# A new order of all recorded steps in a fused attention and gated-MLP kernel

## The chip, the core and the metric

The kernel runs on one core of one Trainium2 chip. The metric is the device time of one execution in microseconds (us), taken on the chip. The core has five engines that work side by side, each through its own queue of instructions and in that queue's order: TensorE (PE in the profile; its weight loads are listed apart as PEld), VectorE (DVE), ScalarE (ACT), GpSimd (POOL) and SyncE (SP). Transfers are started by two queues here: SP starts "hardware" DMAs (q1 in the profile), POOL starts "software" DMAs (q0), and both are carried by the same 16 DMA engines of the core. POOL also computes; a POOL instruction that waits holds up every load that stands behind it.

## The reference

Four batches of 768 rows, 8 heads of 64, go through windowed attention with four sink columns; the result, with heads laid side by side (512 columns), goes through a gated MLP whose gate mixes rows.

```python
scores = q @ k.T / 8                      # per batch and head, 768 x 768
keep = (col < 4) | ((row - col >= 0) & (row - col < 128))
a = softmax(where(keep, scores, -1e9))
x = (a @ v) as [batch, 768, 512]
h = gelu_tanh(x @ w_in)                   # w_in 512 x 1024
u, v = h[..., :512], h[..., 512:]
v_n = (v - mean) / sqrt(var + 1e-6) * g_ln
v_s = w_sg @ v_n + b_sg                   # w_sg 768 x 768, mixes rows
out = x + (u * v_s) @ w_out               # w_out 512 x 512
```

Only tiles on the diagonal of the score matrix, the tiles next to it and the sink columns are computed.

## The kernel before, in words

The kernel is a list of short step names, the string `STEPS`. A loop at the end of the kernel goes through it and calls the function of each name; each function records a few instructions, and no scheduler reorders them. So the place of a step in the list fixes its place in the queue of every engine that it uses, and nothing but data dependencies, buffers coming free and these queues decides when it runs. A step's numbers are, as a rule, batch, then head pair or tile group; a last letter names the engine (A ScalarE, D VectorE, P GpSimd).

How one batch goes through:

- **Loads.** Batch 0's q and k come in four head pairs each, by SP, as plain float32 (`LPQ`, `LPK`, 384 KB each, line 245), and are cast to bfloat16 by a compute engine (`CPQ`, `CPK`, lines 199, 200 and 204). Batches 1 to 3 have q and k loaded and cast by POOL's DMAs, six tiles of 128 rows each (`LQ`, `LK`, line 225); every batch's v comes in two halves by POOL (`LVH`, line 271, 384 KB each, four heads a half). The weights are POOL's loads too: `LW.0` and `LW.1` are the two halves of w_in (line 277), `LWS` the halves of w_sg, `LB` the bias, `LWO` w_out. `LC` brings the sink rows of v by SP.
- **Turns.** q and k have to be transposed. `TQ` and `TK` do it on TensorE into PSUM (lines 376 and 382), and `EQ`, `EK` copy the result to SBUF. For batch 0 a turn is one head pair over all rows; for batches 1 and 2 it is two tiles of rows. Batch 3's six turns are DMA transposes on SP instead (`DQ`, `DK`, line 440).
- **Attention.** `QK` computes the scores of one head pair and one third of the rows (line 483; a biased one adds the mask with line 478), `EX` exponentiates (line 488), `MK` masks on VectorE (line 495) or GpSimd (lines 498 and 501), `KS`, `SK` and `SX` do the sink columns, `AV` multiplies with v (lines 524 to 531), `NR` divides by the row sums. `SK` reads the turned q of all four head pairs.
- **Between.** x is transposed for the MLP: `XT` with the copy `XE` for batch 0, DMA transposes `XD` on SP (line 557) for the others.
- **MLP.** `MV` and `MU` compute the two halves of h (lines 566 and 607), `GV` and `GU` are the gelu, `BN`, `RS`, `NM`, `Z` the normalisation, `SP` the row mixing (line 627), `GT` and `GM` the gate, `OU` or `OH` the output product (lines 644 and 657), `RA` or `RH` add x, `ST` and `SH` store by SP.
- **Fillers.** `HM.n` puts n matmuls on zeros ahead of the next PSUM tile; `TBL` touches ScalarE so that its function table is loaded at that place.

Rings of buffers bound how far an engine may run ahead: two for scores, four for other PSUM tiles, two each for q, k and v. Batch 2 takes the q, k and v buffers of batch 0. A DMA semaphore is used again by the eighth software DMA after it, which waits for the earlier one to land.

The start of the two queues that transfers hang on, and of TensorE's, before:

```
POOL  MASK VSK IDEN CPK.1.P LVH.0.0 LVH.0.1 CPK.3.P LQ.1.0 LQ.1.1 LW.0 LK.1.0 LW.1 MK.0.2.1.P ...
SP    LPQ.0 LPK.0 LPK.1 LPQ.1 LPQ.2 LG LPK.2 LPK.3 LPQ.3 LC ...
PE    TQ.0.0 TK.0.0 QK.0.0.0 QK.0.0.1.1 QK.0.0.2.1 TK.0.1 TQ.0.1 TQ.0.2 QK.0.1.0 QK.0.1.1.1 TK.0.2 TK.0.3 TQ.0.3 ...
```

Of the kernel before, what the change touches and what calls it, by code (L numbers as in the profile page):

```python
# [25 lines left out]
MK.0.1.0.D SX.0.1 SX.0.2 QK.0.3.1 MK.0.2.1.P GCP.D NR.0.0.0 EX.0.3.0 AV.0.0.1 AV.0.1.0 AV.0.1.1 NR.0.0.1 EX.0.3.1
QK.0.1.2 NR.0.1.0 AV.0.2.0 AV.0.3.0 EX.0.1.2 MK.0.3.1.P NR.0.1.1 QK.0.2.2 AV.0.2.1 NR.0.2.0 EX.0.2.2 TQ.1.0 NR.0.3.0
MK.0.1.2.P QK.0.3.2 AV.0.3.1 EQ.1.0.A NR.0.2.1 XT.0.0 NR.0.3.1 LWS.0 AV.0.0.2 EX.0.3.2 TBL.G AV.0.1.2 XE.0.0.D LK.1.1
XT.0.1 MK.0.2.2.D MV.0.0 XE.0.1.A LK.1.2 NR.0.0.2 MK.0.3.2.D LK.1.3 NR.0.1.2 AV.0.2.2 AV.0.3.2 LQ.1.2 NR.0.2.2 GV.0.0
MV.0.1 NR.0.3.2 LQ.1.3 BN.0.0 LWS.1 XT.0.2 GV.0.1 MU.0.1 XE.0.2.A BN.0.1 WT.0 GU.0.1 TK.1.0 MV.0.2 RS.0.1 EK.1.0.A  # L30
LK.1.4 NM.0.1 WE.0.A WT.1 GV.0.2 LK.1.5 TK.1.1 MU.0.2 LB.P EK.1.1.A BN.0.2 Z.0.0.A LK.2.0 WT.2 GU.0.2 MU.0.0 WE.1.D
RS.0.2 WE.2.D Z.0.1.A LQ.2.0 NM.0.2 Z.0.2.A Z.0.3.D Z.0.4.D WT.3 LQ.2.1 WT.4 GU.0.0 TBL.E WE.3.D WT.5 LQ.1.4 Z.0.5.D
TQ.1.1 QK.1.0.0 EQ.1.1.D QK.1.1.0 LQ.1.5 SP.0.0.0 WE.4.D LK.2.1 EX.1.0.0 VSM.1 SP.0.0.1 WE.5.D EX.1.1.0 LVH.1.0
GT.0.0.0 TK.1.2 KS.1 GT.0.0.1 QK.1.2.0 QK.1.3.0 EX.1.2.0 SP.0.0.2 LVH.1.1 GM.0.0.0.D EX.1.3.0 MK.1.2.0.D TQ.2.0
EK.1.2.A LQ.2.2 QK.1.0.1 EQ.2.0.D QK.1.1.1 TQ.1.2 EX.1.0.1 GT.0.0.2 LWO SP.0.0.3 EQ.1.2.D EX.1.1.1 LK.2.2 MK.1.0.1.D
TK.2.0 MK.1.0.0.D QK.1.2.1 LK.2.3 EK.2.0.A QK.1.3.1 MK.1.3.0.D SK.1.0 GM.0.0.1.D LQ.2.3 SP.0.1.0 EX.1.2.1 GT.0.0.3
MK.1.1.0.D LQ.2.4 EX.1.3.1 SP.0.1.1 MK.1.1.1.D LQ.2.5 MK.1.2.1.D SX.1.0 QK.1.0.2 QK.1.1.2 GT.0.1.0 EX.1.0.2 GM.0.0.2.P
SP.0.1.2 GT.0.1.1 EX.1.1.2 LK.2.4 GM.0.1.0.D AV.1.0.0 MK.1.3.1.D AV.1.1.0 LK.2.5 GM.0.0.3.D QK.1.2.2 GT.0.1.2 QK.1.3.2
EX.1.2.2 SP.0.1.3 NR.1.0.0 MK.1.1.2.P EX.1.3.2 NR.1.1.0 AV.1.2.0 AV.1.3.0 MK.1.0.2.P GT.0.1.3 QK.2.0.0 QK.2.1.0
NR.1.2.0 EX.2.0.0 OU.0.0 MK.1.2.2.P NR.1.3.0 TK.2.1 RA.0.0 AV.1.0.1 XD.1.0 EK.2.1.A MK.1.3.2.P AV.1.1.1 NR.1.0.1  # L40
AV.1.2.1 EX.2.1.0 GM.0.1.2.P NR.1.1.1 AV.1.3.1 NR.1.2.1 QK.2.2.0 LK.3.0 QK.2.3.0 EX.2.2.0 OU.0.1 NR.1.3.1 GM.0.1.3.P
EX.2.3.0 TBL.G OU.0.2 XD.1.1 RA.0.1 GM.0.1.1.P TK.2.2 MK.2.3.0.D TQ.2.1 LVH.2.0 TQ.2.2 EQ.2.1.D MV.1.0 EQ.2.2.D LQ.3.0
EK.2.2.D LQ.3.1 VSM.2 MU.1.0 GV.1.0 MK.2.1.0.D LVH.2.1 BN.1.0 MV.1.1 GU.1.0 LQ.3.2 RA.0.2 LQ.3.3 MK.2.0.0.D MV.1.2
GV.1.1 MK.2.2.0.D LK.3.1 KS.2 LK.3.2 BN.1.1 MU.1.1 GV.1.2 LK.3.3 BN.1.2 RS.1.1 MU.1.2 GU.1.1 LQ.3.4 NM.1.1 Z.1.0.A
RS.1.2 OU.0.3 GU.1.2 TBL.E LQ.3.5 NM.1.2 Z.1.1.D SK.2.0 Z.1.4.D QK.2.0.1 Z.1.2.D Z.1.3.A QK.2.1.1 Z.1.5.D OU.0.4
RA.0.3 DK.3.0 SP.1.0.0 RA.0.4 SX.2.0 EX.2.0.1 SP.1.0.1 GT.1.0.0 DQ.3.0 EX.2.1.1 GM.1.0.0.D SP.1.1.0 MK.2.0.1.P
GT.1.0.1 QK.2.2.1 ST.0.3 GT.1.1.0 QK.2.3.1 GM.1.0.1.P DQ.3.1 EX.2.2.1 AV.2.0.0 SP.1.1.1 MK.2.1.1.D EX.2.3.1 MK.2.2.1.P
NR.2.0.0 AV.2.1.0 QK.2.0.2 DQ.3.2 QK.2.1.2 KS.3 EX.2.0.2 MK.2.3.1.P NR.2.1.0 SP.1.1.2 GT.1.1.1 EX.2.1.2 OU.0.5
MK.2.0.2.P GT.1.1.2 ST.0.0 ST.0.4 QK.2.2.2 RA.0.5 QK.2.3.2 MK.2.1.2.P EX.2.2.2 AV.2.2.0 AV.2.3.0 NR.2.2.0 SP.1.1.3
EX.2.3.2 NR.2.3.0 QK.3.0.0 MK.2.3.2.P QK.3.1.0 GT.1.1.3 XD.2.0 EX.3.0.0 AV.2.0.1 MK.2.2.2.D AV.2.1.1 EX.3.1.0 NR.2.0.1  # L50
AV.2.2.1 GM.1.1.3.P ST.0.1 NR.2.1.1 AV.2.3.1 ST.0.2 ST.0.5 GM.1.1.0.P SK.3.0 NR.2.2.1 QK.3.2.0 QK.3.3.0 NR.2.3.1
EX.3.2.0 GM.1.1.2.P SP.1.0.2 EX.3.3.0 XD.2.1 SP.1.0.3 GT.1.0.2 SX.3.0 TBL.G MK.3.3.0.D MV.2.0 GM.1.0.2.P DK.3.1
GM.1.1.1.D LK.3.4 MK.3.0.0.D OU.1.3 LVH.3.0 GV.2.0 OU.1.4 RA.1.3 LVH.3.1 OU.1.5 ST.1.3 RA.1.4 GT.1.0.3 MV.2.1 ST.1.4
MK.3.1.0.D LK.3.5 BN.2.0 GM.1.0.3.P MV.2.2 GV.2.1 BN.2.1 MU.2.1 GV.2.2 BN.2.2 RS.2.1 MU.2.0 GU.2.1 NM.2.1 RA.1.5
RS.2.2 MU.2.2 GU.2.0 NM.2.2 Z.2.4.D Z.2.5.D Z.2.0.A Z.2.1.D OU.1.0 GU.2.2 TBL.E Z.2.2.D MK.3.2.0.D OU.1.1 RA.1.0
Z.2.3.D QK.3.0.1 QK.3.1.1 RA.1.1 SP.2.0.0 EX.3.0.1 DK.3.2 EX.3.1.1 OU.1.2 MK.3.0.1.P GT.2.0.0 ST.1.5 VSM.3 ST.1.0
QK.3.2.1 ST.1.1 QK.3.3.1 EX.3.2.1 SP.2.1.0 GM.2.0.0.D MK.3.1.1.P RA.1.2 EX.3.3.1 SP.2.0.1 ST.1.2 MK.3.3.1.P QK.3.0.2
GT.2.0.1 QK.3.1.2 EX.3.0.2 SP.2.1.1 GT.2.1.0 MK.3.2.1.P EX.3.1.2 GM.2.1.0.D SP.2.1.2 GT.2.1.1 GM.2.0.1.D AV.3.0.0
MK.3.1.2.P GT.2.1.2 AV.3.1.0 NR.3.0.0 AV.3.2.0 AV.3.3.0 MK.3.0.2.P NR.3.1.0 QK.3.2.2 QK.3.3.2 EX.3.2.2 SP.2.0.2
NR.3.2.0 NR.3.3.0 EX.3.3.2 TBL.G SP.2.0.3 MK.3.2.2.P GT.2.0.2 XD.3.0 AV.3.0.1 GT.2.0.3 MK.3.3.2.P AV.3.1.1 NR.3.0.1  # L60
AV.3.2.1 GM.2.0.3.P NR.3.1.1 AV.3.3.1 SP.2.1.3 GM.2.0.2.D GM.2.1.1.P NR.3.2.1 OU.2.0 NR.3.3.1 GT.2.1.3 XD.3.1 OU.2.1
RA.2.0 GM.2.1.3.P OU.2.2 GM.2.1.2.D SH.2.0.0 SH.2.0.1 RA.2.1 MV.3.0 RA.2.2 SH.2.1.0 SH.2.1.1 OU.2.3 GV.3.0 OU.2.4
BN.3.0 MV.3.1 RA.2.3 RA.2.4 MV.3.2 SH.2.3.0 SH.2.3.1 GV.3.1 SH.2.2.0 SH.2.2.1 SH.2.4.0 SH.2.4.1 BN.3.1 OU.2.5 GV.3.2
MU.3.2 BN.3.2 RS.3.1 MU.3.1 GU.3.2 NM.3.1 RS.3.2 NM.3.2 Z.3.0.D Z.3.1.A MU.3.0 Z.3.2.D Z.3.3.A Z.3.4.A Z.3.5.D RA.2.5
SH.2.5.0 SH.2.5.1 SP.3.1.0 GU.3.0 SP.3.1.1 GU.3.1 GT.3.1.0 SP.3.1.2 GM.3.1.0.D GT.3.1.1 SP.3.1.3 GM.3.1.1.D GT.3.1.2
# [650 lines left out]
```

## Time and profile before

The median of three runs is 155.65 us (155.44 to 155.72). The execution that was profiled took 155.89 us; its span from the first to the last instruction is 154.2 us, so 1.7 us lie around the span.

| stretch of the span, us | what runs there | TensorE busy | VectorE | ScalarE | GpSimd |
|---|---|---|---|---|---|
| 0 to 24 | attention of batch 0, first loads | 21.05 of 24 | 16.59 | 19.63 | 17.06 |
| 24 to 55 | MLP of 0, attention of 1 | 30.74 of 31 | 26.32 | 27.90 | 26.21 |
| 55 to 90 | MLP of 1, attention of 2 | 33.63 of 35 | 29.72 | 23.39 | 30.50 |
| 90 to 124 | MLP of 2, attention of 3 | 33.84 of 34 | 29.54 | 20.95 | 22.25 |
| 124 to 150 | MLP of 3 | 25.95 of 26 | 19.61 | 8.15 | 3.67 |

Busy times of an engine say whether it had an instruction in flight; for TensorE they also hold short fillings of the pipeline. The granted clock of TensorE is 1.00 in all stretches.

### The profile page before, as it was taken

To read this page: it belongs to the slowest core of one execution; us is meant where nothing else is said; L and a number is where in the kernel's file an instruction comes from. 1 tells how busy PE (TensorE), PEld (TensorE's weight loads), DVE (VectorE), ACT (ScalarE), POOL (GpSimd) and SP (SyncE) were. 2 spreads that over 40 slices of the span, in tenths; PEclk is the share of its full clock that TensorE was granted. 3 is DMA by queue.
4 is the path that set the end of the run, shared out by engine and by line. 5 is a ranking of instruction groups with operands and counts; after the bars stand their busy time and mean duration, and the time that the engine had idled before them with its cause. 6 is when DMAs were issued, how large, how long until landed. Compare 5 with 4: busy or idle time off the path is not lost.

```text
span 154.2 us, 3867 instructions
## 1 busy us (share of the span) xinstructions
PE 145.7 (95%) x1540; PEld 94.5 (61%) x1554; DVE 122.9 (80%) x296; ACT 100.0 (65%) x117; POOL 99.7 (65%) x127
## 2 busy tenths in 40 slices
PE   6899899999999988999899999999999999999990
...
DMA  4999999999999999999999399996510582410055
GB/s 158 305 351 157 154 195 204 166 189 211 148 141 154 185 155 140 147 150 156 156 223 250 81 276 177 185 190 81 211 72 1 105 221 73 150 54 20 0 203 206
DMA packets 87178, 24.67 MB, mean 160 GB/s; under 512 B 78772, under 2 KB 84920, under 8 KB 87160
## 3 DMA queue, kind: packets, MB, share of 16 engines
...
q14 instruction: 6, 0.05, 0.1%
...
## 4 chain that ended last, share of the span: by engine, by line
PE 54%; POOL 18%; DMA 15%; ACT 4%; DVE 4%; issue 2%; SPq 1%; DVEq 0%; ACTq 0%; POOLq 0%
PE mm L627 15%; DMA v_sb<-in_v_dram 11%; PE mm L644 10%; PE sc L566 9%; PE sc L607 8%; POOL q L225 5%; POOL k L225 4%; DMA uT<-in_k_dram 4%; PE sc L483 4%; PE mm L524 3%; POOL v_sb L271 3%; PE mm L528 2%; POOL wsg_gated L637 2%; POOL P L498 2%; POOL P L501 2%
## 5 line engine op out<-in xcount | busy, mean ns | idle before, releaser
L488 ACT ACTIVATE P<-sc 128x1024 bf16<-128x1024 f32 (+1 forms) x48 | 43.4, 952 | 10.3 <-PE sc L483 10.1
L627 PE MATMUL mm<-wsgT,z 128*128 128x384 bf16 x192 | 34.4, 327 | 0.3 <-ACT z L597 0.3
L627 PEld LDWEIGHTS <-z 128*128 128x128 bf16 x192 | 17.6, 98 | 12.5 <-issue 0.7
L570 ACT ACTIVATE vt<-sc 128x1024 f32<-128x1024 f32 x12 | 12.3, 1027 | 18.4 <-PE sc L566 18.4
L632 DVE SCALAR_TENSOR_TENSOR gtmp<-mm,g_sb,b_bc 128x384 bf16<-128x384 f32 x32 | 19.0, 610 | 4.2 <-PE mm L627 4.0
L637 POOL TENSOR_TENSOR wsg_gated<-gtmp,uT 128x384 bf16<-128x384 bf16 x15 | 14.9, 1006 | 11.3 <-DVE gtmp L632 11.2
L607 PE MATMUL sc<-xT,w_in_sb 128*128 128x256 bf16 x192 | 22.1, 273 | 0.0
L566 PE MATMUL sc<-w_in_sb,xT 128*128 128x512 bf16 x92 | 21.8, 379 | 0.2
L644 PE MATMUL mm<-w_out_sb,wsg_gated 128*128 128x512 bf16 x85 | 21.2, 379 | 0.5
L498 POOL TENSOR_SCALAR_AFFINE_SELECT P<-P 128x512 bf16<-128x512 bf16 x21 | 13.7, 653 | 11.4 <-ACT P L488 11.4
L607 PEld LDWEIGHTS <-w_in_sb 128*128 128x128 bf16 x192 | 18.7, 98 | 2.9
L579 DVE BATCH_NORM_STATS2 st<-vt 128x6 f32<-128x512 f32 x24 | 15.4, 685 | 6.1 <-ACT vt L570 6.0
L541 DVE TENSOR_TENSOR x_sb<-mm,rcp 128x384 bf16<-128x384 f32 (+1 forms) x36 | 18.5, 513 | 1.2
L588 POOL TENSOR_TENSOR rs<-rs,neg_half 128x4 f32<-128x4 f32 (+1 forms) x8 | 7.1, 882 | 15.8 <-DVE rs L583 14.4
L225 POOL DMA_DIRECT2D k<-in_k_dram x18 | 16.4, 924 | 1.3 <-DMA v_sb<-in_v_dram 1.3
L648 DVE TENSOR_TENSOR ot<-mm,x_sb 128x512 f32<-128x512 f32 x23 | 15.4, 683 | 2.2 <-PE mm L644 2.2
L225 POOL DMA_DIRECT2D q<-in_q_dram x18 | 16.8, 956 | 0.0
L524 PE MATMUL mm<-v_sb,P 128*128 128x65 bf16 x192 | 16.1, 194 | 0.6 <-DVE x_sb L541 0.4
L524 PEld LDWEIGHTS <-P 128*128 128x128 bf16 x192 | 14.5, 97 | 2.5 <-DMA v_sb<-in_v_dram 0.6
L528 PE MATMUL mm<-v_sb,P 128*128 128x65 bf16 x160 | 15.4, 193 | 0.4 <-POOL P L501 0.4
L612 ACT ACTIVATE uT<-sc 128x1024 bf16<-128x1024 f32 x12 | 12.2, 1024 | 5.1 <-PE sc L607 5.1
L566 PEld LDWEIGHTS <-xT 128*128 128x128 bf16 x96 | 9.2, 98 | 10.1
...
## 6 DMA issues: line engine op xcount, KB each, us to landing
...
```

Source lines behind the costliest of these rows:

```text
L225: return nc.gpsimd.dma_start(out=dst.rearrange("p (h d) -> p h d", h=H), in_=heads(src, b, i))
L488: nc.scalar.activation(out=P.new((b, p, g))[:, :, 0:w], in_=sc_ring[b, p, g][:, :, 0:w], func=AF.Exp, scale=scale)
L498: nc.gpsimd.affine_select(out=p4[:, :, :, 0:128], in_=p4[:, :, :, 0:128], compare_op=ALU.is_ge, fill=0.0, base=0, pattern=[[0, 2], [0, 2], ...
L524: nc.tensor.matmul(av[:, il, hl, :], pt[:, hl, c:c + 128], vb[:, h, i, :], start=first, stop=False)
L528: nc.tensor.matmul(av[:, il, hl, :], pt[:, hl, c:c + 128], vb[:, h, i - 1, :], start=False, stop=(i < 2 and il == n - 1 and hl == 1))
L541: nc.vector.tensor_mul(x_sb.get(b)[:, i0:i0 + n, 128 * p:128 * (p + 1)].rearrange("p t (h d) -> p t h d", h=2), av[:, :, :, 0:Dh], rcp[:, ...
L566: nc.tensor.matmul(hp[:, jl, :], xT[b][:, 2 * g + jl, c, :], w_in_sb[:, c, d_half:2 * d_half], start=(c == 0), stop=(c == KD - 1))
L607: nc.tensor.matmul(hp[:, dc // 2, 256 * (dc % 2):256 * (dc % 2 + 1)], w_in_sb[:, c, 128 * dc:128 * (dc + 1)], xT[b][:, 2 * g:2 * g + 2, c, :],
L627: nc.tensor.matmul(ps[:, 0:NH], z[b][:, si, 128 * dc:128 * (dc + 1)], wsgT[:, si, NH * hf:NH * (hf + 1)], start=(si == 0), stop=(si == NT ...
L632: nc.vector.scalar_tensor_tensor(out=gtmp.new((b, hf, dc)), in0=mm_ring["g", b, hf, dc][:, 0:NH], scalar=g_sb[:, dc:dc + 1], in1=b_bc[:, N ...
L637: (nc.vector if e == "D" else nc.gpsimd).tensor_mul(gated(b, hf)[:, dc, :], gtmp[b, hf, dc], uT[b][:, dc, NH * hf:NH * (hf + 1)])
L644: nc.tensor.matmul(ps, gated(b, hf)[:, dc, 128 * tl:128 * (tl + 1)], w_out_sb[:, dc, :], start=(dc == 0), stop=(dc == KU - 1))
```

## The change

Every step stays, but for `HM` fillers (21 matmuls in six places before, 19 in eight places after) and the place and number of `TBL`. The whole list stands in another order, and the last letter of some steps changes, which moves a copy, a mask or a product to another engine. What the two transfer queues and TensorE begin with, after:

```
POOL  MASK IDEN LVH.0.0 LVH.0.1 LQ.1.0 LQ.1.1 LW.0 LK.1.0 CPQ.3.P VSK LW.1 LQ.2.0 LK.1.1 MK.0.3.1.P ...
SP    LPQ.0 LPK.0 LPQ.1 LPK.1 LPQ.2 LPK.2 LG LPK.3 LPQ.3 LC ...
PE    TQ.0.0 TK.0.0 QK.0.0.0 QK.0.0.1.1 TQ.0.1 TK.0.1 QK.0.0.2.1 TQ.0.2 TK.0.2 QK.0.1.1.1 QK.0.1.0 TK.0.3 GTR QK.0.2.1 TQ.0.3 QK.0.2.0 SK.0.1 SK.0.2 QK.0.3.1 QK.0.3.0.1 AV.0.0.0 ...
```

Further on, POOL's loads of the third and fourth batch, before and after (compute steps between them left out):

```
before  LK.2.0 LQ.2.0 LQ.2.1 ... LK.2.1 LVH.1.0 LVH.1.1 LQ.2.2 LWO LK.2.2 LK.2.3 LQ.2.3 LQ.2.4 LQ.2.5 LK.2.4 LK.2.5 LK.3.0 LVH.2.0 LQ.3.0 LQ.3.1 LVH.2.1 LQ.3.2 LQ.3.3 LK.3.1 LK.3.2 LK.3.3 LQ.3.4 LQ.3.5 LK.3.4 LVH.3.0 LVH.3.1 LK.3.5
after   LK.2.3 LK.1.4 LVH.1.0 LK.2.1 LK.2.0 LVH.1.1 LWO LQ.2.4 LK.2.2 LQ.3.3 LQ.2.3 LQ.2.5 LQ.2.2 LK.3.2 LQ.3.4 LQ.3.0 LQ.3.5 LK.3.3 LQ.3.1 LK.3.0 LK.2.4 LK.2.5 LVH.2.0 LQ.3.2 LK.3.1 LVH.2.1 LK.3.5 LVH.3.1 LK.3.4 LVH.3.0
```

and SP's queue from the first transpose on:

```
before  XD.1.0 XD.1.1 DK.3.0 DQ.3.0 ST.0.3 DQ.3.1 DQ.3.2 ST.0.0 ST.0.4 XD.2.0 ST.0.1 ST.0.2 ST.0.5 XD.2.1 DK.3.1 ST.1.3 ST.1.4 DK.3.2 ...
after   XD.1.0 XD.1.1 ST.0.2 DK.3.0 DQ.3.0 DK.3.1 DQ.3.1 DQ.3.2 ST.0.4 ST.0.3 ST.0.5 XD.2.0 ST.0.1 XD.2.1 ST.0.0 DK.3.2 ...
```

The diff, cut to the start of the list and to the two functions that it touches:

```diff
-WARM LPQ.0 FILL LPK.0 LPK.1 LPQ.1 LPQ.2 LG MASK LPK.2 LPK.3 CPQ.0.A VSK LPQ.3 IDEN CPK.0.A IDEN2 MASK0 HM.9 TQ.0.0
-TK.0.0 EQ.0.0.D EK.0.0.A VSO HM.4 QK.0.0.0 ZERO CPK.1.P QK.0.0.1.1 EX.0.0.0 LVH.0.0 EX.0.0.1 QK.0.0.2.1 CPQ.1.D TK.0.1
-EX.0.0.2 LC CPQ.2.D LVH.0.1 TQ.0.1 MK.0.0.0.D EK.0.1.A HM.1 TQ.0.2 EQ.0.1.D EQ.0.2.A HM.3 QK.0.1.0 CPK.2.A CPK.3.P
-QK.0.1.1.1 EX.0.1.0 LQ.1.0 CPQ.3.D TK.0.2 EX.0.1.1 TK.0.3 EK.0.2.D LQ.1.1 TQ.0.3 EK.0.3.A GTR EQ.0.3.D LW.0 HM.1
...
+WARM LPQ.0 FILL ZERO MASK LPK.0 IDEN CPQ.0.A IDEN2 MASK0 LPQ.1 LVH.0.0 LPK.1 LPQ.2 HM.8 TQ.0.0 CPK.0.A LPK.2 HM.1
+TK.0.0 LVH.0.1 EQ.0.0.A EK.0.0.A HM.4 QK.0.0.0 EX.0.0.0 CPQ.1.D CPK.1.D LQ.1.0 CPQ.2.D QK.0.0.1.1 LQ.1.1 LW.0 EX.0.0.1
+MK.0.0.0.D LG TQ.0.1 LPK.3 CPK.2.D EQ.0.1.A LPQ.3 TK.0.1 QK.0.0.2.1 EK.0.1.A EX.0.0.2 TQ.0.2 TK.0.2 CPK.3.D QK.0.1.1.1
+QK.0.1.0 LK.1.0 EQ.0.2.A EX.0.1.1 LC TK.0.3 EK.0.2.D EX.0.1.0 EK.0.3.D CPQ.3.P KS.0 VSK VSO GTR QK.0.2.1 GCP.D TQ.0.3
...
-    def TBL(func):
+    def TBL(func, turn):
...
-        ps = mm_ring["o", b, t] if h else fresh(mm_ring, ("o", b, t))
+        ps = mm_ring["o", b, t] if ("o", b, t) in mm_ring.held else fresh(mm_ring, ("o", b, t))
```

`TBL`'s new number is not used; it only keeps the step names apart. In `OH` whichever half comes first takes the PSUM tile; after the change the right half of the last tile does.

More of the change, by code (lines that the diff above doesn't have):

```diff
@@ L26 @@
[L26 to L65, printed above, removed]
@@ L66 @@
-SP.3.0.0 GM.3.1.2.D SP.3.0.1 GT.3.0.0 GT.3.1.3 SP.3.0.2 GT.3.0.1 GM.3.1.3.P SP.3.0.3 GM.3.0.0.D GM.3.0.1.P GT.3.0.2
-OU.3.3 GM.3.0.2.D GT.3.0.3 OU.3.4 GM.3.0.3.D RA.3.3 OU.3.0 RA.3.4 ST.3.3 OU.3.1 RA.3.0 ST.3.4 OU.3.2 ST.3.0 RA.3.1
-OH.3.5.0 OH.3.5.1 ST.3.1 RA.3.2 ST.3.2 RH.3.5.0 SH.3.5.0 RH.3.5.1 SH.3.5.1
+WARM LPQ.0 FILL ZERO MASK LPK.0 IDEN CPQ.0.A IDEN2 MASK0 LPQ.1 LVH.0.0 LPK.1 LPQ.2 HM.8 TQ.0.0 CPK.0.A LPK.2 HM.1
+TK.0.0 LVH.0.1 EQ.0.0.A EK.0.0.A HM.4 QK.0.0.0 EX.0.0.0 CPQ.1.D CPK.1.D LQ.1.0 CPQ.2.D QK.0.0.1.1 LQ.1.1 LW.0 EX.0.0.1
@@ new lines @@
+MK.0.0.0.D LG TQ.0.1 LPK.3 CPK.2.D EQ.0.1.A LPQ.3 TK.0.1 QK.0.0.2.1 EK.0.1.A EX.0.0.2 TQ.0.2 TK.0.2 CPK.3.D QK.0.1.1.1
+QK.0.1.0 LK.1.0 EQ.0.2.A EX.0.1.1 LC TK.0.3 EK.0.2.D EX.0.1.0 EK.0.3.D CPQ.3.P KS.0 VSK VSO GTR QK.0.2.1 GCP.D TQ.0.3
+HM.1 QK.0.2.0 EQ.0.3.D HM.1 SK.0.1 SK.0.2 EX.0.2.1 EX.0.2.0 QK.0.3.1 MK.0.1.0.D LW.1 QK.0.3.0.1 SX.0.2 VSM.0 SX.0.1
+AV.0.0.0 AV.0.1.0 LQ.2.0 AV.0.0.1 LK.1.1 EX.0.3.1 HM.1 AV.0.0.2 MK.0.2.0.D EX.0.3.0 QK.0.1.2 NR.0.0.0 NR.0.1.0
+NR.0.0.1 QK.0.2.2 AV.0.1.1 EX.0.1.2 HM.2 AV.0.2.0 MK.0.3.1.P QK.0.3.2 AV.0.3.0 NR.0.0.2 MK.0.2.1.P NR.0.1.1 MK.0.1.2.P
@@ new lines @@
+NR.0.2.0 EX.0.2.2 AV.0.2.1 EX.0.3.2 NR.0.3.0 NR.0.2.1 AV.0.3.1 NR.0.3.1 XT.0.0 XE.0.0.D TQ.1.0 HM.1 AV.0.1.2 XT.0.1
+MK.0.3.2.P LWS.0 AV.0.3.2 LK.1.2 EQ.1.0.A MK.0.2.2.D AV.0.2.2 LQ.2.1 MV.0.0 NR.0.1.2 LK.1.3 XE.0.1.D GV.0.0 MV.0.1
+LWS.1 NR.0.2.2 NR.0.3.2 XT.0.2 GV.0.1 XE.0.2.A LQ.1.5 BN.0.0 VSM.1 MU.0.1 TK.1.0 MV.0.2 GU.0.1 GV.0.2 MU.0.2 WT.0
+LQ.1.3 BN.0.1 RS.0.1 NM.0.1 LB.P Z.0.3.D BN.0.2 LQ.1.4 EK.1.0.D WT.1 Z.0.2.A Z.0.0.D LQ.1.2 WT.2 LK.1.5 KS.1 RS.0.2
+NM.0.2 MU.0.0 Z.0.1.A Z.0.4.D TBL.G.1 TQ.2.0 GU.0.2 LK.2.3 WE.0.A TK.1.1 WE.2.D Z.0.5.D WE.1.A WT.3 LK.1.4 GU.0.0
@@ new lines @@
+LVH.1.0 SP.0.0.0 EQ.2.0.D QK.1.1.0 EX.1.1.0 EK.1.1.D WE.3.D QK.1.0.0 SP.0.0.1 GT.0.0.0 GT.0.0.1 EX.1.0.0 LK.2.1 WT.5
+WT.4 QK.1.3.0 QK.1.2.0 LK.2.0 LVH.1.1 TQ.1.2 WE.5.D LWO WE.4.A EX.1.3.0 TQ.1.1 LQ.2.4 SP.0.0.2 EQ.1.1.D EX.1.2.0
+QK.1.0.1 QK.1.1.1 EQ.1.2.D GM.0.0.1.D SP.0.0.3 MK.1.3.0.D LK.2.2 EX.1.0.1 MK.1.1.0.D GT.0.0.2 EX.1.1.1 TK.1.2 SK.1.0
+QK.1.2.1 MK.1.0.1.P GM.0.0.0.D QK.1.3.1 GT.0.0.3 EK.1.2.D SP.0.1.0 EX.1.2.1 MK.1.1.1.P EX.1.3.1 MK.1.2.1.D SP.0.1.1
+MK.1.3.1.P SX.1.0 LQ.3.3 TBL.E.1 GT.0.1.0 GT.0.1.1 QK.1.0.2 QK.1.3.2 AV.1.1.0 GM.0.0.2.D TK.2.0 LQ.2.3 SP.0.1.2
```

32 lines of the change are left out of this document (31 added, 1 removed).

## The prediction

> **What bounds the kernel now.** I read the page first, then the chain of waits, then the transfers and the timeline of the first 24 us. The page:
>
> ```profile
> span 154.2 us, 3867 instructions
> ...
> PE 145.7 (95%) x1540; PEld 94.5 (61%) x1554; DVE 122.9 (80%) x296; ACT 100.0 (65%) x117; POOL 99.7 (65%) x127
> ...
> PE   6899899999999988999899999999999999999990
> ...
> DMA  4999999999999999999999399996510582410055
> ```
>
> TensorE is busy 145.7 of 154.2 us, and its idle time is at the two ends; from 24 to 150 us it is idle for 1.8 us in all (126 us less 30.74 + 33.63 + 33.84 + 25.95). So a new order can gain little in the middle, and what delays the start delays everything behind it, unless a later wait absorbs it, and there is hardly one. The DMA engines are full from 4 us to some 88 us. The chain at the start:
>
> ```profile
> 1.81 5.80 DMA uT<-in_k_dram
> ...
> 7.69 0.79 POOL k L204
> 8.48 8.04 DMA v_sb<-in_v_dram
> 16.52 0.04 issue
> 16.56 0.25 PE mm L524 x3
> ```
>
> Start and length in us: SP's third load (batch 0's second k pair), its cast on POOL, which POOL's queue has ahead of the first v half, then that half. Beside this, ScalarE works through copies and exponentials without a gap; the end of that row, with the last q pair's cast and the first v halves:
>
> ```profile
> 8.48 3.26 POOL L271 DMA_DIRECT2D v_sb<-in_v_dram  x2
> 12.85 0.56 DVE L200 CAST q<-z 128x768 bf16<-128x768 f32 x1 [0.85 <-DMA z<-in_q_dram]
> ...
> 17.54 2.64 ACT L488 ACTIVATE P<-sc 128x768 bf16<-128x768 f32 x3
> 20.35 1.02 ACT L488 ACTIVATE P<-sc 128x1024 bf16<-128x1024 f32 x1 [0.17 <-PE sc L483]
> ...
> 22.16 1.04 ACT L488 ACTIVATE P<-sc 128x1024 bf16<-128x1024 f32 x1
> ```
>
> So eight SP pair loads (3.15 MB) all land before POOL's loads get the engines: the eighth at 12.8 us, the first v half at 16.5, and the sixth POOL load (k, issued 15.5) at 23.8.
>
> How the two queues share shows where both are full. Transfers (packets, MB, share of 16 engines) in four windows: SP's q1 alone at 8 to 10 us, POOL's q0 alone at 102 to 104, both at 97.2 to 100 (two 256 KB stores against k and v loads), and 1.0 to 5.9:
>
> ```profile
> q1 hardware_dynamic: 545, 0.78, 105.5%
> ...
> q0 software_dynamic: 2464, 0.31, 245.5%
> ...
> q0 software_dynamic: 2264, 0.29, 164.2%
> q1 hardware_dynamic: 146, 0.27, 29.8%
> ...
> q1 hardware_dynamic: 791, 1.15, 76.5%
> ```
>
> Alone, SP's queue moves 272 packets a us (545 / 2.0), POOL's 1232. Together it is 52 and 809: SP keeps 0.19 of its pace, POOL 0.66. That is 15 POOL packets (256 B read) to one of SP's. SP's queue, not POOL's, gives way.
>
> **The change, part by part.**
>
> *The start of POOL's queue.* Before, both v halves stood behind `CPK.1.P`, which waits until 7.7 us. After, POOL has only `MASK` and `IDEN` ahead of them (POOL is through with these and `VSK` at 3.5 us before, 0.4 us of it `VSK`), so the first half is issued at about 3.2 us. Before, it was issued at 8.48 and the 10.4 to 11.0 window shows no software packet yet; at the same 2.7 us after the issue, software packets run from 5.9 us on. By then SP has moved 1.15 MB and has 2.0 MB, five loads, to go: 5.1 us at its pace alone (0.39 MB a us). Behind the v halves POOL issues two q tiles, half of w_in and a k tile without a wait, before `CPQ.3.P` blocks it for SP's last pair. Alone these six take 11.4 us: 3.2 for a v half (the last two landed 3.2 apart), 0.83 for a q or k tile (40.52 to 44.62 us: five in 4.1), 2.5 for w_in. The engines have no room for both: 5.9 + 5.1 + 11.4 = 22.4 us until all are in, as against 23.8 for the same fourteen loads before. What changes is who is last. At 0.19 of its pace SP would move 3.3 of its 5.1 us worth while POOL's 11.4 take 17.3, so SP's eighth load lands last, at 22.4 (24.7 if sharing loses pace, as 0.19 + 0.66 < 1 says). The other end is that it lands at 12.8 as before. I take 22, by the row with both queues full, since it is the same two queues on the same engines.
>
> *What waits for it.* TensorE's queue has `TQ.0.3` (through `CPQ.3.P`) ahead of `QK.0.2.0`, both `SK` and every `AV` of batch 0, and `TK.0.2` (through the sixth load) ahead of both first `QK.0.1`; none can be overtaken. From the landing to `MV.0.0`, the first matmul of the MLP: cast on POOL 0.83, `TQ.0.3` 0.4, `QK.0.2.0` 0.3, then ScalarE `EX.0.2.0` 0.81, two `SX` 0.8, `EX.0.3.1` 1.02, `EX.0.3.0` 0.81, three `EX` of the last third 3.06, then `MK.0.3.2.P` 1.28 and the two `AV` ahead of `MV.0.0` 0.9: 10.2 us, durations from the same steps' rows. 22 + 10.2 = 32.2 against 23.4 before: 8.8 later. Before, two `AV` (0.9) still came after `MV.0.0`; net 7.9. As a check, 12.8 + 10.2 = 23.0 with an unhurt load, so the rest of the start is worth 0.4 + 0.9 at most.
>
> *Copies that change engines.* ScalarE has eight copies ahead of the first gelu before and after; `XE.0.1` (1.0) goes to VectorE. `EQ.0.0` moves to ScalarE in front of `EK.0.0` (0.8 serial, was parallel), but the first `QK` waits only 0.2 longer, as k's own pair sets it. All of it is idle time while the loads are late: nothing. Two fillers fewer, 0.4 us, likewise. `TBL` moved: the table load (1.28) stands in the queue without a wait of its own either way: nothing.
>
> *POOL's later loads* are held by `CPQ.3.P` and by `LQ.2.0`, which waits for `TQ.0.3` to free batch 0's q buffer; so they shift with the start and keep their distance from their users. The k tile between w_in's halves costs 0.83 of DMA ahead of `LW.1`, which `MU.0.1` needs 6 us later than it lands.
>
> *Batch 2 and 3.* `LK.2.4` and `LK.2.5` come after eight loads of batch 3 q and k, but `TK.2.2` moves behind `MU.1.1` and `OU.0.3`, some 10 us of TensorE: it loses the 0.5 wait that it has now. Ten loads in a row hold `GM.0.1.0.P` about 10 us (0.92 each, v 1.45), and `OU.0.4` has 11.8 us of matmuls ahead: covered by 2, and if that cover is gone `RS.1.1` behind it and the row mixing are late by as much. Five turns in a row on SP (1.3 to 1.9 each to issue) meet `LVH.2.1`; `AV.2.3.0` needs it: 0 to 1.5. Batch 3's v last has 7 us in hand before `AV.3.1.0`. `XD.2.1` gets 5.0 us of matmuls in place of 6.9 between the last `AV` and `MV.2.1`, with 5.7 needed: 0.7. The last MLP has 10.4 us of matmuls from `MV.3.0` to the row mixing in place of 11.3, with 11.4 of chain: 0.5. Against these stand waits that go, 1.1 at `TK.2.1` and an `AV` near 58 us. Sum of the middle: 0, bounds -1.8 (all idle time) and +3.
>
> Sum: 155.9 (the profiled execution, 154.2 + 1.7 around the span) + 7.9 + 0 = 163.8. That execution is 0.25 above the median, so 163.5.
>
> A rule of the Trainium skill speaks against this. DMA: Bandwidth & Descriptors, in Queues, rings and completion order, says that an engine takes turns between queues by whole packets, some 9 to 17 descriptors each. If SP's turns held as many as POOL's, its large rows would lose little; the shared window agrees with such turns for POOL alone (15 to one). The first rival is what the rule gives if it holds for both.
>
> **The rivals.** *SP's loads keep their pace* (ends on the other side: faster). Turns of one packet each cost SP 59 ns (16 / 272) in 72 (13 more, 16 / 1232), 1.2 times 5.1 us, 1.1 later than now at most, and the v halves come 2 us earlier. For it: the two queues overlap at 11 to 12.8 us now, and SP's last load still lands 1.0 after the one before. Against: 52 packets a us with stores, and at 11 only leftovers run. The start is then 1.3 better at best and 0.2 worse at worst, the middle 0 to -0.5: 154.9. It decides if the eighth load lands before 14 us. *Half pace*: loads share better than stores do. 2.0 MB at 0.195 MB a us lands at 16.2, `MV.0.0` at 26.4, net 2.1: 157.8. *The start is unhurt but the five turns starve `LVH.2.1`* and `XD.2.1` is late: 1.5 + 0.7 + 0.5 less 0.5: 157.8 too, with the waits after 75 us. That the edit does nothing cannot be: the program's order of POOL is as above.
>
> **How the numbers follow.** SP squeezed: 0.70, 163.5, own range 159.5 to 167 (landing at 18 to 24.7, middle -0.5 to +0.8). Pace kept: 0.15. Half pace: 0.10. Late turns: 0.05. The range 156.5 to 167 leaves out most of the second case and little above. Within 0.2% (155.34 to 155.96), about what a measurement of this kernel can tell from no change: 0.04, from the second case; faster 0.13; slower 0.83.
>
> **What would show it.** Right: software packets from about 6 us, SP's eighth load landing beyond 18, TensorE in its 40 slices with low digits in slices 2 to 6, POOL waiting in line 204 for a q pair for 8 us or more, `MV.0.0` (line 566) near 32, and from there the same distances as before. Wrong: the eighth load before 14 us and line 566 near 23; or line 566 near 23 and new idle time of TensorE at line 524 or 566 after 75 us.

## The result, and the profile after

The changed kernel takes 162.42 us in the median of four runs (162.0 to 163.0); the kernel before, beside it on the same chip, 155.69 us (155.44 to 156.11). The ratio is 1.043, with a 95% interval of 1.039 to 1.047. The execution that was profiled took 163.0 us, with a span of 161.3. In the experiments below, medians count every execution and ratios leave out those over 1.5% above the fastest of the same kernel, to which the profiled executions of experiments 3 (164.71 us) and 5 (162.62) belong.

So the direction and the size were as forecast (163.5). The place was not: most of the loss lies between 53 and 72 us, a stretch for which the sum had 0, and the start, for which it had 7.9, gave about 1.5. The page after:

```profile
span 161.3 us, 3859 instructions
...
PE 147.7 (92%) x1537; PEld 95.2 (59%) x1552; DVE 127.5 (79%) x302; ACT 99.3 (62%) x116; POOL 96.3 (60%) x124
...
PE   6698999999999958499989999999999999999990
...
PEclk9999999999999999969999999999999999999998
```

A slice is 4.03 us. The forecast wanted low digits of TensorE in slices 2 to 6; slice 2 has a 6 (8 before) and slices 3 to 6 have 9, 8, 9, 9. The low ones are 5, 8, 4 in slices 15 to 17 (56 to 69 us), and the granted clock falls once ahead of the end, in slice 18. The table by stretch says the same. Columns: stretch and its length, busy time of TensorE with its instructions, granted clock, share of the DMA engines, GB/s. First the kernel after:

```profile
24.00:53.00 29.00, 28.89 (x335) 1.00 1.99 179
53.00:74.00 21.00, 16.20 (x168) 0.92 1.63 130
```

and the second of these stretches in the kernel before:

```profile
53.00:74.00 21.00, 19.79 (x215) 1.00 2.04 150
```

To put numbers on the places I added up TensorE's matmul time step by step and compared when each kernel had done the same amount. The lag of the kernel after, us:

| reached in the kernel after at about, us | 15.9 | 26.9 | 43 | 55.8 | 60.1 | 67.0 | 72.5 | 91 | 124 | 155 |
|---|---|---|---|---|---|---|---|---|---|---|
| lag | 1.0 | 1.3 | 1.4 | 1.6 | 3.4 | 5.6 | 7.1 | 7.0 | 6.8 | 6.85 |

The start gives some 1.5, the stretch from 55.8 to 72.5 us gives 5.5, and everything after it, with all the later terms of the sum, gives -0.2 net. That is 6.85; the two spans differ by 7.1. Of the 5.5 us, 1.5 fall between 67.0 and 72.5 us, where the clock is halved (see below).

**The start.** The first v half was issued at 3.17 us, as the order says, and `CPQ.3.P` blocked GpSimd's queue for 4.34 us (columns: start, length, what, and the wait ahead of it with what ended it):

```profile
14.02 0.83 POOL L204 TENSOR_SCALAR q<-z 128x768 bf16<-128x768 f32 x1 [4.34 <-DMA z<-in_q_dram]
```

The eighth load of SP had landed at 13.93, against 12.82 before and 22 in the forecast. The transfers of the kernel after from 9 to 12 us (packets, MB, share of 16 engines) show how the two queues shared:

```profile
q1 hardware_dynamic: 608, 0.87, 92.1%
q0 software_dynamic: 543, 0.07, 35.1%
```

That is 203 packets a us for SP's queue and 181 for GpSimd's. From 9.5 to 12 us it is 492 and 482 packets: one for one, where the window with stores that the forecast went by had 52 and 809 a us. One for one is the premise of the first rival. The Trainium skill, DMA: Bandwidth & Descriptors, section Queues, rings and completion order, has an engine take turns between queues by whole packets. The trace agrees with such turns of equal size here; the stores' window, at one to 15, does not. Moreover, no software packet moved from 5.9 to 8.4 us: the first came at about 8.6, some 5.5 us after its issue (2.6 in the kernel before), so the two queues met 2.7 us later than forecast.

In this execution the eighth load was not even what TensorE waited for. Its cast was through at 14.85, and `TQ.0.3`, which needs it, began at 15.54, behind a `QK` that waited for ScalarE:

```profile
15.21 0.40 PE L483 MATMUL sc<-qT,kT 64*128 64x256 bf16 x6 [0.67 <-ACT P L488]
```

From there the chain goes back through ScalarE to the first k pair, cast at 6.64 us (5.02 before). The start also differs from trace to trace. Of all traces of this document, the seven with the changed start have the eighth load at 13.47 to 15.05 us and `MV.0.0` at 24.53 to 26.07; the five with the start of the kernel before have 12.79 to 13.71 and 23.40 to 24.42. So the changed start is later in each of them, by 0.1 to 2.7 us, and 1.5 is this trace's figure.

**The middle.** The chain that ended last, from 53 to 74 us of the kernel after (start, length, what):

```profile
54.99 2.50 DVE P L495
...
58.33 0.56 DVE x_sb L541
...
58.91 7.62 DMA xT<-x_sb
...
66.58 2.48 PE sc L607 x16
```

The 2.50 us are the mask `MK.1.3.2.D`, which the change took from GpSimd to VectorE and put ahead of `NR.1.3.0` and `NR.1.2.0`. The second of these (58.33) makes the last rows of x that the DMA transpose `XD.1.0` reads. It was issued at 58.91, against 55.49 before, and then took 7.62 us to land, with `MU.1.0` waiting. Beside it, VectorE's and GpSimd's rows and TensorE's wait:

```profile
54.91 2.59 DVE L495 TENSOR_TENSOR P<-P,mask 128x1024 bf16<-128x1024 bf16 x1
55.12 0.66 POOL L498 TENSOR_SCALAR_AFFINE_SELECT P<-P 128x512 bf16<-128x512 bf16 x1
...
56.89 1.10 POOL L501 TENSOR_SCALAR_AFFINE_SELECT P<-P 128x512 bf16<-128x512 bf16 x1
...
58.24 0.81 PE L644 MATMUL mm<-w_out_sb,wsg_gated 128*128 128x512 bf16 x2 [1.78 <-DVE x_sb L541]
```

The same VectorE mask (128 x 1024) takes 0.68 us where GpSimd runs nothing beside it:

```profile
84.75 0.68 DVE L495 TENSOR_TENSOR P<-P,mask 128x1024 bf16<-128x1024 bf16 x1
```

Here it runs beside four GpSimd instructions (two masks of two halves each, the middle two left out above), ends 0.56 us after the third of them is through at 56.94, and the fourth takes 1.10 instead of 0.65. TensorE waited 1.78 us at 56.5 to 58.2 and 2.65 at 63.9 to 66.6, and then had half its clock (granted clock 0.50) from 67.78 to 71.19.

Three things therefore stand in a row: a slow mask, a slow turn, and a half clock. The theory (called Middle in the expectations) says that the mask is the cause and the other two follow; the rivals are the turn's own company of loads, the half clock by itself, and the start (Theory Start: the 1.5 us and the late stage that they lead into).

### The profile page after: what moved, and what is told of

Same layout as the page of the kernel before. It is cut to its first block, busy times and chain, and to the rows that moved or that the text cites. A ratio compares the mean times of both kernels' runs of the same rounds, so it can differ in the third digit from the quotient of the medians.

```text
span 161.3 us, 3859 instructions
## 1 busy us (share of the span) xinstructions
PE 147.7 (92%) x1537; PEld 95.2 (59%) x1552; DVE 127.5 (79%) x302; ACT 99.3 (62%) x116; POOL 96.3 (60%) x124
## 4 chain that ended last, share of the span: by engine, by line
PE 71%; DVE 11%; DMA 8%; ACT 5%; issue 2%; SPq 0%; DVEq 0%
PE mm L627 17%; PE sc L566 12%; PE sc L607 11%; PE mm L644 10%; PE sc L483 6%; DMA xT<-x_sb 5%; PE mm L524 3%; DMA uT<-in_k_dram 3%; DVE P L495 3%; ACT P L488 2%; PE mm L528 2%; PE mm L382 2%; DVE z L600 2%; PE mm L531 2%; DVE st L579 2%
## 5 line engine op out<-in xcount | busy, mean ns | idle before, releaser
L607 PE MATMUL sc<-xT,w_in_sb 128*128 128x256 bf16 x192 | 23.0, 277 | 2.7 <-DMA xT<-x_sb 2.7
L566 PE MATMUL sc<-w_in_sb,xT 128*128 128x512 bf16 x93 | 22.7, 394 | 0.2
L637 POOL TENSOR_TENSOR wsg_gated<-gtmp,uT 128x384 bf16<-128x384 bf16 x13 | 12.4, 962 | 14.5 <-DVE gtmp L632 10.5
L495 DVE TENSOR_TENSOR P<-P,mask 128x768 bf16<-128x768 bf16 (+1 forms) x23 | 16.3, 724 | 0.4 <-ACT P L488 0.4
L566 PEld LDWEIGHTS <-xT 128*128 128x128 bf16 x96 | 9.7, 102 | 11.6 <-issue 1.5
L524 PE MATMUL mm<-v_sb,P 128*128 128x65 bf16 x192 | 16.4, 194 | 0.2
L225 POOL DMA_DIRECT2D q<-in_q_dram x18 | 16.3, 909 | 0.0
L524 PEld LDWEIGHTS <-P 128*128 128x128 bf16 x192 | 14.4, 98 | 2.5 <-issue 0.5
```

The source lines that it names most:

```text
L225: return nc.gpsimd.dma_start(out=dst.rearrange("p (h d) -> p h d", h=H), in_=heads(src, b, i))
L495: nc.vector.tensor_mul(pt[:, :, 0:w], pt[:, :, 0:w], m.unsqueeze(1).to_broadcast([128, 2, w]))
L524: nc.tensor.matmul(av[:, il, hl, :], pt[:, hl, c:c + 128], vb[:, h, i, :], start=first, stop=False)
L566: nc.tensor.matmul(hp[:, jl, :], xT[b][:, 2 * g + jl, c, :], w_in_sb[:, c, d_half:2 * d_half], start=(c == 0), stop=(c == KD - 1))
L607: nc.tensor.matmul(hp[:, dc // 2, 256 * (dc % 2):256 * (dc % 2 + 1)], w_in_sb[:, c, 128 * dc:128 * (dc + 1)], xT[b][:, 2 * g:2 * g + 2, c, :],
```

## The experiments

All are the changed kernel with some names of `STEPS` moved or another engine letter; where the string has become a line shorter, the profile's line numbers are one lower (the masks of line 495 are at 494). "Before" ran beside each group: 155.93 for the first four, 155.83 for the next four, 155.38 for the next three and 155.42 for the last. Ratios are to it. A wait of TensorE is the profile's idle time ahead of the matmul; the expectations count some of them 0.15 us longer.

**1. Fillers against the half clock** (`e1_fill`)

```diff
-NR.1.3.1 MU.1.0
+NR.1.3.1 HM.12 MU.1.0
```

> Twelve filler matmuls ahead of MU.1.0, where TensorE waits 2.8 us for the turned x of batch 1; the rest as in the changed kernel (162.4). Theory Middle (the loss is made from 53 to 72 us: a mask ahead of the row divisions on VectorE, a slow turn by DMA, and then TensorE at half clock for 3.4 us because it stood idle): the fillers (12 x 0.216 = 2.6 us) keep the clock at 1.00 and 1.7 us come back, 160.7. Theory Start (the loss is made by the early v loads): no change, 162.4.

Measured: 162.17 us, 1.039 [1.030, 1.047]. The drop behind `MU.1.0` was gone, but one came at 60.15, behind the first wait (1.78 us), so this run alone decided nothing.

**2. The mask out of the way** (`e2_mask`)

```diff
-NR.1.0.0 MK.1.3.2.D SP.0.1.3 LQ.2.5 AV.1.0.1 EX.1.2.2 NR.1.3.0 NR.1.2.0 XD.1.0 GM.0.0.3.D
+NR.1.0.0 SP.0.1.3 LQ.2.5 AV.1.0.1 EX.1.2.2 NR.1.3.0 NR.1.2.0 XD.1.0 GM.0.0.3.D MK.1.3.2.D
```

> MK.1.3.2.D (2.6 us on VectorE in the changed kernel) moved behind NR.1.3.0, NR.1.2.0 and GM.0.0.3.D. Theory Middle: XD.1.0 is issued some 2.5 us earlier (56.5 in place of 58.9), OU.0.0's wait of 1.8 us goes, the wait for the turn shrinks or goes: 158.5 to 160.5. Theory Start: 162.4.

Measured: 158.47 us, 1.016 [1.009, 1.023], as Theory Middle said: 4 us less for one name moved. The turn was issued at 56.65 and landed 3.8 us later, and the clock stayed full until the end of the kernel. The chain of this run shows what is left (start, length, what):

```profile
57.41 1.32 DVE P L494
...
62.66 5.70 DMA xT<-x_sb
```

The mask, now 1.40 us long with 0.57 us of GpSimd's masks beside it, delays the next normalisations: TensorE waited 1.18 us (58.8 to 60.0) for the buffer that `GT.0.1.3` frees, and the second turn, `XD.1.1`, had become the late one, by 0.66.

**3. The loads beside the turn** (`e3_loads`)

```diff
-AV.1.3.1 LQ.2.2 LK.3.2 OU.0.2 OU.0.1 LQ.3.4 GM.0.1.2.P GM.0.1.3.P
+AV.1.3.1 LQ.2.2 OU.0.2 OU.0.1 GM.0.1.2.P GM.0.1.3.P LK.3.2 LQ.3.4
```

> The batch 3 loads LK.3.2 and LQ.3.4 moved behind GM.0.1.3.P, so that the turn XD.1.0 meets one load in place of three. Theory Middle with the loads as what slows the turn: it lands 4.5 us after its issue in place of 7.6, the wait at MU.1.0 goes (2.8) and the clock stays up (1.7): 158 to 159. Rival inside it, that the turn is slow by itself: still 7 us to land, 162.4. Theory Start: 162.4.

Measured: 162.43 us, 1.040 [1.030, 1.050]. `XD.1.0` took 3.7 us instead of 7.6 (4.5 was expected). But `XD.1.1` then met the loads. Its line in the chain of this run:

```profile
64.72 7.99 DMA xT<-x_sb
```

TensorE waited 2.54 us for it. So a turn is slow where the loads run beside it (7.6 and 8.0 us against 3.7), but with two turns and as many loads to bring, moving two loads only chose which turn paid.

**4. v's halves behind the first k cast** (`e4_vlate`)

```diff
-CPK.1.D
+CPK.1.P LVH.0.0 LVH.0.1      (and no longer ahead of it)
```

> Both v halves of batch 0 behind CPK.1 on POOL, as in the kernel before (CPK.1 goes to POOL for that). Theory Start: the first k pair lands at 5.0 in place of 6.6 us, the eighth at 12.8 in place of 13.9, MV.0.0 starts 1.5 earlier or more: 160.9 or less. Theory Middle: MV.0.0 moves by 0.5 at most and the time stays at 162.0 to 162.8.

Measured: 160.32 us, 1.025 [1.015, 1.034]. The eighth load landed at 12.62, as Theory Start said, yet `MV.0.0` came at 28.26, later than the 25.57 of the changed kernel: `CPQ.3.P` now had six loads' issues of GpSimd ahead of it, TensorE waited 2.41 us for it, until 16.79, and the half clock followed from 18.56 to 21.98. Its chain:

```profile
9.30 1.76 POOL v_sb L270
...
15.87 0.88 POOL q L203
```

The time fell for another reason. With all shifted, GpSimd was issuing a load and not masking when `MK.1.3.2.D` came, the mask took 0.68, the turn 3.8, and the lag stayed at about 4 us from 29 us to the end: the middle lost nothing, and what this start had lost stayed lost. That is for Theory Middle, in a run that was made for another purpose.

**5. The mask on GpSimd, in the same place** (`e5_maskP`)

```diff
-MK.1.3.2.D
+MK.1.3.2.P
```

> The same mask step on GpSimd (MK.1.3.2.P in place of D), its place in the list as in the changed kernel. Theory Middle, with the mask slow only because GpSimd masks at the same time (0.68 us alone, 2.6 beside it): VectorE goes on to NR.1.3.0 at once, XD.1.0 is issued at 56 or before, both waits from 56 to 67 us go, no half clock there: 157.0. Rival: the mask only changes places and the products behind GpSimd's third mask are late instead (GM.0.1.2.P, OU.0.4): 159 or more.

Measured: 160.56 us, 1.028 [1.019, 1.037]; expected was about 157. VectorE was free of this mask, but GpSimd's queue got it in front of its others, and the collision came earlier, at two VectorE masks that stand before it. The chain of this run:

```profile
50.84 3.91 DVE P L494 x2
...
62.87 7.77 DMA xT<-x_sb
```

Two masks in 3.91 us held `AV` back for 2.10 us, and TensorE waited 2.32 us for the second turn. This execution had the half clock twice (from 54.47 and 71.54); experiment 8 shows the same collision without it.

**6. Experiments 4 and 5 together, with the last q cast on VectorE** (`e6_maskP_vlate`)

```diff
-CPK.1.D CPQ.3.P MK.1.3.2.D
+CPK.1.P CPQ.3.D MK.1.3.2.P   (v's halves behind CPK.1.P)
```

> As e5_maskP, and the start's loads as before: CPK.1 on GpSimd with both v halves behind it, and CPQ.3 on VectorE, so that no cast waits behind GpSimd's loads. If the early v loads cost the start (eighth load at 14 to 15 us in place of 12.8, and TQ.0.3 1.7 to 1.9 later): eighth load at 12.7, TQ.0.3 at 14, MV.0.0 near 24 in place of 25.7, and 1.5 less than e5_maskP: 155.5. Rival, that the start is late by its order of casts, masks and matmuls: MV.0.0 at 25.5 or later, 157.

Measured: 164.43 us, 1.055 [1.048, 1.063]. The eighth load was in at 12.97, but `MV.0.0` came at 27.85. With `VSK`'s work on GpSimd (`headsel`, which the sink steps need) behind the loads, and the cast late in VectorE's order, the start was late by its queues, not by its transfers; the half clock from 18.31 to 21.72 added to it. The rival that it named (the order of the casts) held for `MV.0.0`, not for the time (157).

**7. Fillers in both waits** (`e7_fill2`)

```diff
-QK.2.3.0 ... MU.1.0
+HM.9 QK.2.3.0 ... HM.12 MU.1.0
```

> The changed kernel with fillers in both of TensorE's long waits: nine ahead of QK.2.3.0 (in front of the 1.8 us at OU.0.0) and twelve ahead of MU.1.0. If an idle TensorE is what halves the clock: no half clock before 157 us and 160.7. If the clock follows something else: half for 3.4 us somewhere, 162.4.

Measured: 162.56 us, 1.046 [1.038, 1.053]. The clock kept 1.00 through the stretch in which the changed kernel had 0.50. By windows, the changed kernel (columns as above):

```profile
68.00:71.00 3.00, 3.00 (x11) 0.50 1.76 241
```

and this run:

```profile
68.00:71.00 3.00, 2.95 (x20) 1.00 2.21 209
```

The time did not fall. The turn, issued at 58.79, took 8.5 us and landed at 67.30, and `MU.1.0` began 0.76 us later than without fillers. Even so the weights of the last matmul of `MU.1.1` were loaded at 78.43 instead of 79.36, and those of the last `SP` of batch 1 at 96.88 instead of 97.79. Then TensorE waited 0.59 us, to 102.28, for a turn of batch 2 for which the changed kernel does not wait; this execution's span is 161.1 for 161.3. So the half clock follows the waits. Its 3.41 us cost about 1.7 on the spot (0.93 and 0.76), and at the end no more than 0.2 of it was left as a gain.

**8. The start of the kernel before, on experiment 5** (`e8_maskP_start`; all steps up to `MV.0.0` in before's order and on before's engines)

```diff
-WARM LPQ.0 FILL ZERO MASK LPK.0 IDEN CPQ.0.A IDEN2 MASK0 LPQ.1 LVH.0.0 ...
+WARM LPQ.0 FILL LPK.0 LPK.1 LPQ.1 LPQ.2 LG MASK LPK.2 LPK.3 CPQ.0.A VSK LPQ.3 ...
```

> As e5_maskP, with all steps up to MV.0.0 in the order and on the engines that they have in the kernel before. The start's share of the loss by itself: MV.0.0 near 23.4 in place of 25.7, and with the two AV that come ahead of it there 0.9 of work more or less done, 1.5 less than e5_maskP: 155.5. If the loss at the start is recovered later anyway: as e5_maskP.

Measured: 161.4 us, 1.037 [1.029, 1.044]; expected was 155.5. `MV.0.0` was at 24.42, and the middle lost as in experiment 5: two VectorE masks in 3.89 us, and the first turn took 7.8 us. The clock stayed at 1.00 until the end. In the traces the two starts hardly differ (24.53 in experiment 5), so this pair says little of the start's price; it shows that the middle loses as much behind the start of the kernel before.

**9. No GpSimd mask beside it** (`e9_allD`)

```diff
-MK.1.1.2.P ... MK.1.2.2.P
+MK.1.1.2.D ... MK.1.2.2.D
```

> The two GpSimd masks MK.1.1.2.P and MK.1.2.2.P of the changed kernel go to VectorE, at their places in the order; MK.1.3.2.D stays where the change put it, ahead of NR.1.3.0 and NR.1.2.0. So VectorE has more to do than in the changed kernel (two more masks), and GpSimd computes nothing beside MK.1.3.2.D. Theory Middle (the mask was slow because GpSimd masked at the same time): MK.1.3.2.D takes 0.68 to 0.75 us instead of 2.59, OU.0.0 waits under 1 us, XD.1.0 is issued before 57.5 us and MU.1.0 starts before 64.5; 157.5 to 159.5 us. Rival (the order on VectorE alone is too full, whatever GpSimd does): MK.1.3.2.D still ends after 56.8, MU.1.0 starts after 65.5, and the two added masks make it no better: 161.5 to 163.5 us.

Measured: 160.36 us, 1.031 [1.025, 1.036]. This is the direct test of what slows the mask: VectorE has two masks more, `MK.1.3.2.D` stands where the change put it, and nothing masks on GpSimd while it runs. VectorE's wide masks of this stretch in this run's timeline:

```profile
55.28 0.93 DVE L494 TENSOR_TENSOR P<-P,mask 128x1024 bf16<-128x1024 bf16 x1
...
58.49 1.12 DVE L494 TENSOR_TENSOR P<-P,mask 128x1024 bf16<-128x1024 bf16 x1
...
60.06 0.68 DVE L494 TENSOR_TENSOR P<-P,mask 128x1024 bf16<-128x1024 bf16 x1
```

The first is `MK.1.3.2.D`: 0.93 in place of 2.59, beside load issues of GpSimd alone. (The second, 1.12 us, ran beside a GpSimd product of 0.96 us.) `OU.0.0` waited under 0.2 us, `MU.1.0` began at 63.82 instead of 66.57. As the theory said, apart from 0.93 where 0.68 to 0.75 was expected, and an issue of the turn at 57.63 for 57.5. The time was 0.9 above its range: TensorE waited 1.17 us, to 59.67, for an added mask, the second turn was put off to 63.45, it took 6.73 us, and TensorE waited 1.86 for it.

**10 and 11. The start of the kernel before, on experiments 2 and 9** (`e10_mask_start`, `e11_allD_start`; the edit of experiment 8)

> e2_mask (MK.1.3.2.D behind GM.0.0.3.D) with all steps up to MV.0.0 in the order, and on the engines, of the kernel before. If the start costs what its lag shows in e2_mask (1.5 to 1.7 us at MV.0.0) and nothing behind it waits otherwise: 158.5 - 1.0 to 1.6 = 156.8 to 157.5 us, MV.0.0 before 24.6 us. Rival (the start's lag is taken up by a later wait anyway, or before's start needs before's order behind it): 158 to 159.5 us.

Measured: 157.84 us, 1.019 [1.014, 1.023]. `MV.0.0` was at 23.49 and the lag there 0.1. Yet the ratio is that of experiment 2 (1.016) within both intervals, and the time lies between the two that were expected. What the start costs in time, some 1.5 by the trace, is not resolved by these two.

> e9_allD with the start of the kernel before, as in e10_mask_start. If both losses are mended by this and they add: 156 to 157.5 us, 1.0 to 1.6 us below e9_allD. Rival: the start is not worth it here either, within 0.5 us of e9_allD.

Measured: 160.56 us, 1.032 [1.026, 1.038], within 0.2 us of experiment 9: the rival. TensorE waited 2.08 us for the second turn, to 69.42, and the half clock came at 69.49.

**12. The mask one group later still** (`e12_mask2_start`)

```diff
-XD.1.0 GM.0.0.3.D MK.1.3.2.D NR.1.0.1 QK.2.0.0 MK.1.1.2.P GT.0.1.3
+XD.1.0 GM.0.0.3.D NR.1.0.1 QK.2.0.0 MK.1.1.2.P GT.0.1.3 MK.1.3.2.D
```

(against experiment 10)

> e10_mask_start with MK.1.3.2.D one step group later still: behind NR.1.0.1 and GT.0.1.3 instead of ahead of them. In e10_mask_start TensorE waited 1.34 us (57.35 to 58.74) for a PSUM buffer that GT.0.1.3 freed behind that mask. If the mask's place on VectorE is the cause: that wait falls below 0.5 us, the mask takes 0.68 to 0.9 us (GpSimd's masks are over by then), MU.1.0 starts before 61.2 us and the lag to the kernel before at equal TensorE work is under 0.9 us at MU.1.2; 156.3 to 157.3 us. Rival (the wait moves to the next user of the mask, AV.1.3.1, or the second turn XD.1.1 takes it back among the software loads): a wait of over 0.9 us remains between 57 and 68 us more than in e10_mask_start, 157.5 to 158.5 us.

Measured: 156.6 us, 1.007 [1.005, 1.010], 1.2 us below experiment 10, in the expected range. The chain in this run:

```profile
57.68 0.53 DVE gtmp L631
58.20 0.60 DVE P L494
...
61.52 5.58 DMA xT<-x_sb
```

The mask takes 0.68 us, since GpSimd's are over at 57.47, and experiment 10's wait of 1.18 us is gone (`MU.1.0` began at 61.57, expected was before 61.2; 1.82 of lag at `MU.1.2` where under 0.9 was expected). Two parts of that lag show: 1.05 at `MV.0.0`, with the eighth load at 13.71 in this execution, and 1.01 us that TensorE waited for the second turn, issued at 61.52 (before: 59.93) among loads of the fourth batch. The execution in this trace took 157.59 us, like experiment 10's (157.60): its `MV.0.0` came 0.83 us later, and the middle won about as much. No version tried here beats the kernel before.

## Why the prediction was right, and where it was not

**The number was right by luck; its working was not right.** 163.5 was forecast and 162.42 came; but of the 7.9 us for the start some 1.5 are there, and the middle, put at 0 with bounds of -1.8 and +3, lost 5.5. Two errors of opposite sign met. The forecast's own signs fail too: it wanted software packets from 6 us (8.6), the eighth load beyond 18 (13.93), a wait of 8 us or more in line 204 (4.34) and `MV.0.0` near 32 (25.57).

**The start.** The step that failed is the landing of SP's eighth load at 22 us, taken from how the two queues shared at 97 to 100 us. That row had stores in SP's queue; the loads of the start shared one packet for one, and the load landed at 13.93. (That paragraph's 24.7 should also read 25.0 by its own shares: 5.9 + 17.3 + 1.8.) From landing to `MV.0.0` it was 11.6 us for a forecast 10.2, so 25.57 where the same sum gives 24.1; but in this trace `TQ.0.3` did not wait for the landing, and ScalarE's exponentials ahead of it set the start's pace, which the sum had only behind the cast. In four of the other six traces with this start (1, 3, 7 and 9) `TQ.0.3` did wait for the cast, 0.3 to 0.5 us. The first rival had the sharing, and its sign, a landing before 14 us, came in this trace and in experiment 5; in the other five it was 14.4 to 15.05, between that rival and half pace (16.2). Its bound for the start, 0.2 worse, was too small, and its 154.9 fell with the middle. I can't say why stores share 1 to 15 and loads 1 to 1, nor why the first software packet took 5.5 us; no run tried it.

**The middle.** The step that failed is "Sum of the middle: 0, bounds -1.8 (all idle time) and +3". It priced loads, turns and the last stages, but not one mask that changed engine and place. Before, `MK.1.3.2.P` ran on GpSimd behind `XD.1.0`; after, `MK.1.3.2.D` was in VectorE's queue ahead of the two normalisations that `XD.1.0` and `OU.0.0` wait for. By its row of 0.68 it would have cost, as an estimate, under a microsecond. It took 2.59. That it did so because of GpSimd's masks is shown by 9 (0.93 without them), 4 and 12 (0.68), and that this one name carries the largest part by 2 (162.42 to 158.47) and by 10 to 12 (1.2 us more for its last step). Rows of the trace before gave a hint, though not the size. Such a mask took 1.10 and 1.15 us at 79.98 and 87.13, where GpSimd computed beside it; the first, with the GpSimd row:

```profile
79.98 1.10 DVE L495 TENSOR_TENSOR P<-P,mask 128x1024 bf16<-128x1024 bf16 x1
79.62 0.91 POOL L637 TENSOR_TENSOR wsg_gated<-gtmp,uT 128x384 bf16<-128x384 bf16 x1
```

It ended 0.55 us after GpSimd's product, as the 2.59 us one ended 0.56 after GpSimd's third mask: by these rows a mask costs the rest of what GpSimd is doing, and in a row of masks that can be several of them.

**What followed it.** The late turn fell among software loads and took 7.6 us instead of 3.7 to 3.8 (2 and 3). It is the second cause in the chain, not an independent one: with the turn issued in time, or with the loads elsewhere, it lands early, but then the other turn can be the late one (3, 5, 9). The half clock came with the waits. In the row of experiment 7 it cost about 1.7 us on the spot, but little was left at the end. In experiment 1 the two executions at a granted clock of 0.996 and 0.999 took 161.69 and 161.29 us, the two at 0.989 162.65 and 163.07.

**The later terms** were named and small in the forecast (`LVH.2.1` 0 to 1.5, `XD.2.1` 0.7, the last MLP 0.5, against waits of 1.1 that go). Together they came to -0.2 from 72.5 us on. The fourth rival, late turns, did not happen.

**What stays open:** what the start is worth in time (2 and 10 don't resolve it, while in 4 a lag of some 4 us from the start stayed to the end), what the half clock alone costs in the whole, and the last 0.7% of experiment 12, in whose trace the second turn's wait of 1.01 us and a late start are the visible parts; bringing that turn forward was not tried.
